# Routed attention and a SoLU MLP on one core: the first batch's fourth pair loaded in 128-byte runs and turned by VectorE

## The chip, the core and the metric

The kernel runs on one core of a Trainium2 chip: TensorE (PE, with its weight loads PEld), VectorE (DVE), ScalarE (ACT), GpSimd (POOL) and SyncE (SP), which here issues nearly all DMAs. The metric is device microseconds of one execution. The kernel before took 225.69 us, the median of three runs (225.38 to 227.81).

## What is computed

Attention over 4 batches, 8 heads, 768 tokens of 64 numbers, in which a query sees only the keys assigned to the same of 16 clusters, and then a SoLU MLP over the 3072 tokens:

```
q_assign = argmax(q_n @ c_n.T); k_assign = argmax(k_n @ c_n.T)      # 16 clusters per head
scores = where(q_assign[:, None] == k_assign[None, :], (q @ k.T) / sqrt(64), -1e9)
x = softmax(scores) @ v                                             # heads side by side: 3072 x 512
h = x @ w_in                                                        # 512 -> 1024
solu = h * softmax(h)
out = ((solu - mean) / sqrt(var + 1e-6) * g_ln) @ w_out             # 1024 -> 512
```

## The kernel before

**Work items and their written order.** The kernel records every step as a named item with an engine, a planner's cost, a due time and the items it needs (`Weave.add`, L97). The engines' queues are written out by hand as lists of kinds (`ORDER`, L28 to L73): each kind takes the next item of that kind on that engine, and `AWAY` (L74 to L91) moves single items from their default engine to another. `Weave.run` (L124) walks the queues and emits the instructions. Every engine executes its queue in order; an item whose inputs are late holds up all behind it.

**Names.** `b.p` is batch and pair of heads (4 batches, 4 pairs); a further `0` or `1` is q or k.

- `ld` loads one tensor of a pair into `raw` (eight buffers), `lv` loads v, `cv` casts it (three buffers for v, so that lv0.3 waits for cv0.0).
- A pair has to lie with the 64 numbers of a head on partitions. From batch 1 on, `load` (L396) brings 32 x 32 blocks with four DMAs, each row of a block a run of 128 bytes, and `xt` (L404) turns the blocks on DVE by one 32-wise transpose. For batch 0 (`by_token`, L351) the tokens are brought in long runs, one DMA of 1536-byte runs (`load_apart`, L372), turned on PE (`tp`, L382, three transposes of 128 x 128 each) into the PSUM region `hreg`, and copied from there by `xa` (L389) on ACT or DVE. Pair 0.0 is treated in halves (a further `.0` or `.1`).
- `ca` casts the turned tensor to bf16 into the tile `qk` (L423). `cl` multiplies it by the centroids (L438), `tb` turns the result (L456), `mx` takes the maximum over 16 (L465), `oh` compares (L474), `ot` turns the marks back (L487), `pl` copies them below q and k in `qk` (L498), and `bl` clears the rows of the other head (L521). The score matmul then contracts over the 64 numbers and the 16 or 32 marks, so that a pair of the same cluster gets a constant on top, which the exponential takes off again.
- Pairs 0.1 to 0.3 are treated "apart" (`apart`, L355): each head has its own 16 rows of marks, placed by POOL from a wide turned tile, with no `bl`.
- `S` is a bank of scores (L594, ring of three PSUM banks), `E` its exponential on ACT (L604, ring of nine `e` tiles), `V` the product with v for one head and 128 tokens (L615), `N` the division on DVE (L628). In batch 0, units 0 to 3 are pair 0 (six banks of 384 each), and then, three banks of 512 each, 4 to 7 pair 1, 8 to 11 pair 2, 12 to 15 pair 3, and 16 to 21 the last two token blocks of pairs 1, 2 and 3.
- `lo` and `li` load w_out and w_in in slabs of 512 KB; `wi` casts a slab of w_in; `su`, `sk`, `me`, `ce` sum, keep, average and centre w_out, with `lg`, `gt`, `gk`, `sg`, `gs` for g_ln.
- Per block of 128 tokens `f`: `tx` turns x (a DMA), `h` is two of its eight matmuls with w_in into `hreg`, `hm` the maximum, `ex` the exponential, `u` the product, `tu` turns u (a DMA; for the last two blocks `ptu` on PE and copies), `bn`, `ag`, `at`, `al` the statistics, `y` two of the eight matmuls with w_out, `sc` the scaling and `ou` the store. The first `h` needs tx0 and all four `wi`; tx0 needs N6.
- `wm` and `fl` are matmuls on zeros that only keep PE busy at the start; `cp` and `cq` turn the centroids, `cb` and `cf` keep them in two forms, `zo` and `z` clear or fill tiles.

**DMAs.** Each DMA on SP waits for the one eight before it (eight semaphores in turn). Nothing on SP is reordered.

Of the kernel before, what the change touches and what calls it, by code (L numbers as in the profile page):

```python
# [22 lines left out]
class Weave:  # L23
# [18 lines left out]
    """
    ORDER["PE"] = """
        wm tp2 cp tp cl tp fl5 cl fl4 S3 tp2 S2 tp S cq S tp S2 tp2 S2 V3 S cl S tp2 V3 S gt S tp S
        tp S2 cl S2 V2 S V S2 tp S2 tp S2 V2 S V S2 cl S2 V2 S V2 S3 V S2 V2 S2 V S cl S3 su S2 V3 S
        V S3 V3 S2 V S su S2 V S V3 S3 me S3 V4 S3 cl S3 V4 S2 h S h S2 h S h S2 V3 S2 V h S h V S V
        S h S V S V S h S2 V3 S2 V h S2 h V2 S y3 S2 h3 S3 y V3 h V S2 V2 S cl S3 h2 S2 V3 S y2 S V
        h2 S V y2 S h S V h S2 h S y3 S2 y V3 h S3 cl V2 S V S y S2 y2 S3 V3 S y S2 V3 S2 cl S V S2
        V2 S h S2 V2 S V S h S2 V2 cl V2 S3 y2 S V S2 V y S2 y V2 S3 h2 S V h S h S2 V h S V S V y2
        S h V y2 S2 V S h3 S cl V S2 V2 S h V cl S3 h2 V y V S3 y2 V S h V3 S y S h S2 h2 S3 V2 y h  # L50
        S V S2 y V3 y S3 h3 y S3 V3 S h S V S V cl S V S h S cl V2 S3 y V2 S y S2 y V2 S3 h y V S3 V
        h V2 S3 cl S2 V2 S y3 S2 y S V3 S V S y S2 V S V3 S2 y2 S3 y V2 S2 h V2 S3 h3 S V S2 V y S V
        h2 V2 S y S2 y V y S h2 S3 cl h V S2 V3 S h V2 S3 h2 S y S2 V h S2 V y2 V4 S3 y h S2 h V h V
# [9 lines left out]
        bn oh bn xt hm ot ag N cv u bn2 xt hm tb mx u N tb oh mx hm ot bn2 oh ag u N sc ag hm bn ot
        u bn N xt2 ag xt2 hm tb N bl mx tb bn2 oh u N xt ag xt sc hm ot tb mx oh N bn sc N u bn N ag
        xt ot bn ca N mx sc oh hm u bn ag N xt hm bn2 bl tb u ot ag N hm mx bn2 u bn N oh ot hm bl2
        u ag N cv hm sc bn u N hm ag bn N bn u bn2 hm ag2 N bn u bn2 N ag hm bn u N ag hm bn2 u bn2
        hm sc u N ag2 bn tx hm bn sc u bn ag hm bn tu ag u bn2 tu ag sc
# [101 lines left out]
def kernel(  # L169
# [11 lines left out]
    nc = tc.nc  # L181
# [241 lines left out]
    def cast(b, p, i, hh, cols, e):  # L423
        xt, h = xts[b, p, i], 2 * p + hh
        r = rows(h)
        if apart(b, p):
            src, dst = by_two(b, p, i)[r], every_other(b, p, i, hh)[:D]
        else:
            src, dst = xt[r, cols], side(b, p, i, hh, cols)[:D]
        if e == "ACT":  # L430
            nc.scalar.activation(dst, src, Act.Copy, scale=inv_C if i else 1.0)
        elif i == 0:
            VEC[e].tensor_copy(dst, src)  # L433
        else:
            VEC[e].tensor_scalar(dst, src, scalar1=inv_C, scalar2=1.0,  # L435
                                 op0=Alu.mult, op1=Alu.mult)

    def clusters(b, p, hf):  # L438
# [59 lines left out]
    def place(b, p, hf, i, part, e):  # L498
# [355 lines left out]
    add("wm", "PE", 3.55, -1000, lambda e: [idle(FF2) for _ in range(6)])  # L854
# [42 lines left out]
    for idx, (b, p) in enumerate(pairs):  # L897
        first = first_of(b, p)
        if by_token(b):
            for hf, i in ((hf, i) for hf in range(2) for i in range(2)):  # L900
# [5 lines left out]
                add(f"tp{t}.{hf}", "PE", 0.7 - 0.2 * hf if halves_of(b, p) else 0.36, first - 15 + i + hf,  # L906
# [9 lines left out]
        for i in range(2):  # L916
# [3 lines left out]
            if seq >= 8:  # L920
                pb, pp = pairs[(seq - 8) // 2]
                o = (seq - 8) % 2
                free = ([f"tp{pb}.{pp}.{o}.{x}" for x in range(2)] if by_token(pb) else
# [6 lines left out]
            elif by_token(b):  # L930
# [319 lines left out]
```

## Time and profile before

| what | value |
|---|---|
| median of three runs | 225.69 us |
| the profiled execution, its own time | 225.95 us |
| its span, from the first to the last instruction | 223.9 us |
| granted PE clock | 1.00 throughout |
| hreg<-ident_f,raw (tp, L386), 48 matmuls | 8.3 us busy |
| xt<-hreg (xa, L393), 10 on DVE and 6 on ACT | 5.1 and 2.8 us busy |
| xt<-raw (xt, L407), 24 on DVE | 22.6 us busy |
| DMA queue q1, share of 16 engines | 80.6% |
| HBM read and written | 23.11 and 6.29 MB |

Busy shares say how much of the span an engine worked; the stretches say when. A group of instructions has its line, engine, tiles and shape, then total busy time and mean ns of one, then the idle time just before them and what ended it. In the chain of waits each step was released by the one before it. First E at 10.52 us, first h at 46.16, first ex at 50.36.

### The profile page before, as it was taken

The page shows a single profiled execution, that of the slowest core. Times are in us where ns is not written, and L with a number is a line of the kernel's source. Part 1 is how long each engine was busy: PE and PEld are TensorE (multiplying, and loading weights), DVE is VectorE, ACT ScalarE, POOL GpSimd, SP SyncE. Part 2 cuts the span into 40 slices and gives each one's busy share as a digit, 9 for nine tenths or more (in the row PEclk, how much of TensorE's full clock was granted, in tenths as well). Part 3 has the DMA queues.
Part 4 walks back from the last instruction along what each step waited for, and adds up shares of the span by engine and source line. Part 5 has one row for each costly group of instructions (what it writes and reads, how often), then busy time and mean ns, then how long its engine had stood idle before and what let it go on. Part 6 is the DMA issues. An engine that isn't in the chain of part 4 may idle for free.

```text
span 223.9 us, 6574 instructions
## 1 busy us (share of the span) xinstructions
PE 215.1 (96%) x2388; PEld 148.1 (66%) x2420; DVE 197.3 (88%) x359; ACT 191.5 (86%) x371; POOL 127.1 (57%) x247
## 2 busy tenths in 40 slices
PE   7899999999999999999999999999999999999993
PEld 3576756677667678776677667777677687754442
DVE  3799899899999989999998989887998889888981
ACT  3689999999998999998889899999999998982362
POOL 3489843964794999547668634943895413031331
PEclk9999999999999999999999999999999999999999
DMA  7998989999898989999999999199931433766622
GB/s 152 353 318 147 249 199 275 290 243 158 132 199 140 232 130 165 193 189 177 183 218 168 184 195 195 65 174 232 236 64 28 79 70 120 96 146 170 176 97 94
DMA packets 125679, 38.80 MB, mean 173 GB/s; under 512 B 115016, under 2 KB 121168, under 8 KB 125648
## 3 DMA queue, kind: packets, MB, share of 16 engines
q1 hardware_dynamic: 123904, 37.87, 80.6%
q10 hardware_dynamic: 1744, 0.52, 1.0%
q8 instruction: 19, 0.31, 0.6%
q14 instruction: 12, 0.10, 0.2%
HBM read 23.11 MB, written 6.29 MB: 131 GB/s over the span
## 4 chain that ended last, share of the span: by engine, by line
PE 86%; ACT 5%; DVE 3%; issue 3%; DMA 1%; POOL 1%; ACTq 0%; DVEq 0%; POOLq 0%
PE sps L601 28%; PE hreg L710 18%; PE yps L771 16%; PE ops L624 14%; ACT e L607 5%; PE csc L450 4%; PE hreg L386 2%; PE hreg L574 1%; PE hreg L771 1%; DMA c_all<-in_centroids_dram 1%; PE csc L445 1%; DVE bs L738 1%; DVE u L727 1%; ACT xt L393 0%; PE hreg L584 0%
## 5 line engine op out<-in xcount | busy, mean ns | idle before, releaser
L607 ACT ACTIVATE e<-sps 128x512 bf16<-128x512 f32 (+1 forms) x294 | 151.0, 599 | 12.2 <-PE sps L601 10.2
L601 PE MATMUL sps<-qk 80*128 80x256 bf16 (+5 forms) x636 | 93.8, 264 | 1.8 <-POOL qk L514 0.7
L601 PEld LDWEIGHTS <-qk 80*128 80x128 bf16 (+1 forms) x636 | 60.2, 121 | 27.9 <-issue 9.0
L624 PEld LDWEIGHTS <-e 128*128 128x128 bf16 x1152 | 50.4, 97 | 12.3 <-issue 1.9
L624 PE MATMUL ops<-v,e 128*128 128x65 bf16 x1152 | 55.0, 193 | 0.1
L710 PE MATMUL hreg<-w_in_sb,xT 128*128 128x512 bf16 x173 | 49.1, 379 | 1.1
L771 PE MATMUL yps<-w_out_c,uT 128*128 128x512 bf16 x171 | 46.4, 379 | 0.6
L727 DVE TENSOR_TENSOR u<-e_sb,hreg 128x1024 bf16<-128x1024 bf16 x24 | 29.0, 1210 | 4.9 <-ACT e_sb L722 4.7
L514 POOL COPY qk<-oht 32x384 f32<-32x384 f32 (+1 forms) x50 | 24.4, 488 | 15.8 <-DVE oht L494 13.6
L738 DVE BATCH_NORM_STATS2 bs<-u 128x6 f32<-128x512 bf16 x48 | 31.5, 676 | 0.2
L716 DVE TENSOR_REDUCE nmax<-hreg 128x1 f32<-128x1024 f32 x24 | 29.0, 1209 | 2.6 <-PE hreg L710 2.2
L722 ACT ACTIVATE e_sb<-hreg,nmax 128x1024 bf16<-128x1024 f32 x24 | 26.9, 1120 | 4.5 <-DVE nmax L716 4.4
L433 POOL CAST qk<-xt 64x768 bf16<-64x768 f32 (+1 forms) x31 | 26.1, 842 | 5.5 <-DVE xt L393 3.9
L771 PEld LDWEIGHTS <-uT 128*128 128x128 bf16 x200 | 18.2, 97 | 12.3 <-DVE uT L704 0.7
L754 POOL TENSOR_SCALAR esq<-es,mv 128x1 f32<-128x1 f32 x24 | 8.5, 355 | 29.0 <-DVE mv L742 20.8
L435 POOL TENSOR_SCALAR qk<-xt 64x768 bf16<-64x768 f32 (+1 forms) x28 | 23.0, 820 | 1.7
L710 PEld LDWEIGHTS <-xT 128*128 128x128 bf16 x192 | 16.8, 97 | 9.4 <-issue 0.6
L407 DVE STREAM_TRANSPOSE xt<-raw 128x768 f32<-128x768 f32 x24 | 22.6, 953 | 0.2 <-DMA raw<-in_q_dram 0.2
L748 POOL TENSOR_SCALAR es<-esum 128x1 f32<-128x1 f32 x24 | 5.3, 221 | 27.6 <-ACT e_sb L722 27.1
L649 DVE TENSOR_TENSOR x<-ops,den 128x256 bf16<-128x256 f32 (+1 forms) x39 | 18.9, 486 | 1.3
L757 POOL TENSOR_TENSOR alpha<-esq,halves 128x1 f32<-128x1 f32 x24 | 13.5, 561 | 2.0
L786 ACT ACTIVATE y<-yps,alpha 128x512 f32<-128x512 f32 x13 | 9.0, 692 | 6.4 <-PE yps L771 6.0
(80 smaller groups left out, 170.1 us busy)
## 6 DMA issues: line engine op xcount, KB each, us to landing
vf<-in_v_dram SPq DMA_DIRECT2D x16, 384.0 KB, 4.4
out_dram<-y SPq DMA_DIRECT2D x23, 256.0 KB, 2.7
raw<-in_q_dram SPq DMA_DIRECT2D x50, 96.0 KB, 3.7
raw<-in_k_dram SPq DMA_DIRECT2D x50, 96.0 KB, 3.0
w_g<-in_moe_w_out_dram SPq DMA_DIRECT2D x4, 512.0 KB, 5.3
w_st<-in_moe_w_in_dram SPq DMA_DIRECT2D x4, 512.0 KB, 5.9
raw<-in_q_dram SPq DMA_DIRECT2D x3, 384.0 KB, 6.3
raw<-in_k_dram SPq DMA_DIRECT2D x3, 384.0 KB, 6.8
```

What stands on the lines that cost most here:

```text
L433: VEC[e].tensor_copy(dst, src)
L435: VEC[e].tensor_scalar(dst, src, scalar1=inv_C, scalar2=1.0, op0=Alu.mult, op1=Alu.mult)
L514: ins = VEC[e].tensor_copy(dst.bitcast(F32), src.bitcast(F32).unsqueeze(1) .to_broadcast([NB, 2, n // 2]))
L601: nc.tensor.matmul(sps_[n, k][:, c0:c0 + w], side(b, h // 2, 1, h % 2, keys)[r], side(b, h // 2, 0, h % 2, slice(s0 * P, s0 * P + w))[r])
L607: nc.scalar.activation(es[n, k][:, :w], sps_[n, k][:, :w], Act.Exp, scale=exp_scale, bias=-exp_scale)
L624: nc.tensor.matmul(opss[g][:, s, :VW], es[n, k][:, c0:c0 + P], v1[slot(b, h // 2)][:, h % 2, kt, :VW], start=(kt == 0), stop=(kt == n_t - 1))
L710: uses(nc.tensor.matmul(hreg[:, at(f, f2)[1], :], xTs[f][:, dc, :], w_in_sb[:, dc, f2 * FF2:(f2 + 1) * FF2], start=(dc == 0), stop=(dc == ...
L716: uses(nc.vector.tensor_reduce(ff[f, "nmax"][:], pair_of(f), axis=AXY, op=Alu.max, negate=True), *both(f))
L722: uses(nc.scalar.activation(ff[f, "e"][:], pair_of(f), Act.Exp, bias=ff[f, "nmax"][:], accum_out=ff[f, "esum"][:]), *both(f))
L727: uses(nc.vector.tensor_tensor(ff[f, "u"][:], ff[f, "e"][:], pair_of(f), op=Alu.mult), *both(f))
L738: nc.vector.bn_stats(ff[f, "bs"][:, f2, :], ff[f, "u"][:, f2, :])
L771: ins = nc.tensor.matmul(dst, ff[f, "uT"][:, at(f, f2)[0] * (n_fc // 2) + c, :], w_out_c[:, fc, cols], start=(fc == 0), stop=(fc == n_fc - 1))
```

## The change

1. Pair 0.3 is taken out of the way of batch 0 (`by_pe` is true only for pairs 0 to 2 of batch 0). It is loaded like the later batches, in eight DMAs of 32 x 32 blocks (98 KB each) instead of two of 393 KB, turned on DVE by two `xt` instead of twelve PE transposes and four copies, and treated with 32 rows of marks and a `bl` instead of apart. Its tokens keep the order of batch 0: its `ca` and its `cl` read every sixth column of the turned tile. (The old helper `by_pe` is renamed `by_product`.)
2. `pl` of pair 0.0 may also run on ACT; three of them do (pl0.0.0.1.1, pl0.0.1.0.0, pl0.0.1.0.1).
3. All five written orders and the list `AWAY` are new. One `fl` less stands on PE (8 for 9). `sk` goes to ACT, `wi3` to DVE, three more `sc` to ACT, four more `pl` of batches 2 and 3 to SP.

The beginnings of the orders, with the kinds resolved to items:

```
SP   before: ld0.0 (4) lv0.0 si ld0.1.0 ld0.1.1 ld0.2.0 ld0.2.1 lv0.1 lg ld0.3.0 ld0.3.1 ld1.0.0.0 ld1.0.0.1
             lv0.2 lv0.3 ld1.0.0.2 ld1.0.0 ld1.0.1.0 ld1.0.1.1 lo0 lo1 ... lo2 ... lo3 ... ld1.1.1 li0-3 tx0
SP   after:  ld0.0 (4) lv0.0 si lv0.1 ld0.1.0 lg ld0.1.1 ld0.2.0 lv0.2 ld0.2.1 ld0.3.0.0-2 lo0 ld0.3.0
             ld0.3.1.0-2 ld0.3.1 ld1.0.0.0-1 lo1 ... lo2 ... lo3 ld1.1.0.2 ld1.1.0 lv0.3 ... ld1.1.1 li0-3 tx0
DVE  before: cn cb xa0.0.0.1 ca0.0.1.0.0 tb0.0.0 mx oh ot pl0.0.0.1.1 pl0.0.0.0.0 tb0.0.1 mx oh ot xa0.1.0.0 ...
DVE  after:  cn cb tb0.0.0 mx oh ot pl0.0.0.1.0 pl0.0.0.0.0 tb0.0.1 mx oh ot pl0.0.1.1.0 xa0.1.0.0 xa0.1.0.1
             xa0.1.1.0 xa0.1.1.1 cf tb0.1 mx oh ot gk N0 xa0.2.0.1 xa0.2.1.0 pl0.1.0.0 xt0.3.0 xt0.3.1 tb0.2
             mx oh ot N1 tb0.3 cv0.2.1 pl0.2.1.1 N2 xt1.0.0 xt1.0.1 mx0.3 N3 oh0.3 ot0.3 tb1.0 ...
ACT  before: wa xa0.0.0.0 xa0.0.1.0 ca0.0.0.0.0 ca0.0.0.1.1 xa0.0.1.1 ca0.0.1.0.1 ca0.0.1.1.0 E0.0 (9 E)
             E1.3 E1.4 E1.5 xa0.2.1.0 xa0.2.1.1 (6 E) xa0.3.0.0 E3.0 ...
ACT  after:  wa xa0.0.0.0 xa0.0.1.0 xa0.0.0.1 xa0.0.1.1 ca0.0.0.0.1 pl0.0.0.1.1 ca0.0.1.1.0 E0.0 (9 E)
             pl0.0.1.0.0 pl0.0.1.0.1 E1.3 E1.4 E1.5 xa0.2.0.0 (8 E) xa0.2.1.1 E3.2 ... E13.0 sk E13.1 ...
POOL before: po z1 ca0.0.0.0.1 ca0.0.0.1.0 pl0.0.0.1.0 pl0.0.0.0.1 cv0.0.1 z2 bl0.0.0 ...
POOL after:  po ca0.0.0.0.0 ca0.0.0.1.0 ca0.0.0.1.1 ca0.0.1.0.0 zo pl0.0.0.0.1 bl0.0.0 ca0.0.1.0.1 cv0.0.0 ...
PE   before: ... S0.0 S0.1 S0.2 tp0.1.0.0 tp0.1.0.1 S1.0 S1.1 tp0.1.1.0 S1.2 cq ... S13.1 su1 ... S15.1 me
             ... S19.0 h0.0.0 ... y22.0 y22.1 ptu23.0 ptu23.1 y22.2 y22.3 y23
PE   after:  ... S0.0 S0.1 S0.2 cq S1.0 tp0.1.0.0 S1.1 S1.2 tp0.1.0.1 ... S13.0 su1 S13.1 S13.2 S14.0 me
             ... S19.1 h0.0.0 ... y22.0 y22.1 y22.2 ptu23.0 ptu23.1 y22.3 y23
```

At the end ACT copies both halves of u23 (before, DVE copied the second, behind bn23), and DVE both of u22.

The diff without the orders, cut to its core:

```diff
+    def by_pe(b, p):
+
+        return by_token(b) and p < 3
+
     def apart(b, p):
-        return by_token(b) and not halves_of(b, p)
+        return by_pe(b, p) and not halves_of(b, p)
...
         if apart(b, p):
             src, dst = by_two(b, p, i)[r], every_other(b, p, i, hh)[:D]
+        elif by_token(b) and not by_pe(b, p):
+            src = xt[r].rearrange("p (n t) -> p t n", t=n_t)
+            dst = side(b, p, i, hh, cols)[:D].rearrange("p (t n) -> p t n", t=n_t)
...
-            nc.tensor.matmul(csc[c * NB:(c + 1) * NB, :n], c_bd[:, p, :],
-                             xts[b, p, i][:, lo + part * n:lo + (part + 1) * n],
+            x = xts[b, p, i][:, lo + part * n:lo + (part + 1) * n]
+            if by_token(b) and not by_pe(b, p):
+                x = xts[b, p, i][:].rearrange("p (n t) -> p t n", t=n_t)[
+                    :, part * (n_t // 2):(part + 1) * (n_t // 2)]
+            nc.tensor.matmul(csc[c * NB:(c + 1) * NB, :n], c_bd[:, p, :], x,
                              tile_position=(0, c * NB))
...
+        elif e == "ACT":
+            ins = nc.scalar.copy(dst, src.unsqueeze(1).to_broadcast([NB, 2, n]))
...
-        if by_token(b):
+        if by_pe(b, p):
             for hf, i in ((hf, i) for hf in range(2) for i in range(2)):
...
-            elif by_token(b):
+            elif by_pe(b, p):
                 add(f"ld{t}", "SP", 0.55, first - 40 + i,
                     (lambda e, b=b, p=p, i=i: load_apart(b, p, i)),
...
-            if by_token(b):
+            if by_pe(b, p):
                 kept = [[f"xa{t}.{hf}"] for hf in range(2)]
```

Three of the planner's costs change with it (`wm`, `tp` of pair 0.0, `pl` on ACT); the queues are written out, so these move no instruction.

More of the change, by code (lines that the diff above doesn't have):

```diff
@@ L63 @@
[L63 to L67, printed above, removed]
+        cn cb tb mx oh ot pl2 tb mx oh ot pl xa4 cf tb mx oh ot gk N xa2 pl xt2 tb mx oh ot N tb cv
@@ L999 @@
                 e = ("DVE", "POOL")[j % 2] if half else "POOL" if apart(b, p) else "SP"
-                costs = ({"DVE": 0.3, "POOL": 0.41} if half else
+                costs = ({"DVE": 0.3, "POOL": 0.41, "ACT": 0.42} if half else
                          {"POOL": 0.76, "DVE": 0.46} if apart(b, p) else
```

98 lines of the change are left out of this document (51 added, 47 removed).

## The prediction

> **What bounds the kernel now.** I read the page's busy times first, then the busy times by stretch, the waits of the first 50 us, the chain of waits around the first scores, the groups by form and last the timelines around the first `h`.
>
> ```profile
> PE 215.1 (96%) x2388; PEld 148.1 (66%) x2420; DVE 197.3 (88%) x359; ACT 191.5 (86%) x371; POOL 127.1 (57%) x247
> ```
>
> PE is the bound over the whole span. But the shares are an average. By stretch (columns: the stretch, its length, PE, weight loads, DVE, ACT and POOL busy with their instructions, clock, DMA share, GB/s):
>
> ```profile
> 10.00:15.00 5.00, 4.84 (x53) 3.98 (x57) 4.74 (x13) 3.76 (x10) 4.03 (x12) 1.00 1.11 356
> 20.00:25.00 5.00, 4.71 (x66) 3.40 (x66) 4.67 (x11) 4.89 (x12) 4.62 (x10) 1.00 0.74 214
> 45.00:50.00 5.00, 4.94 (x69) 3.82 (x68) 4.82 (x9) 5.00 (x11) 3.31 (x6) 1.00 1.24 261
> 80.00:85.00 5.00, 4.95 (x68) 4.07 (x66) 4.80 (x8) 4.75 (x11) 4.52 (x9) 1.00 0.79 125
> ```
>
> From 15 to 60 us ACT runs exponentials at 92 to 100% of the time, and a busy PE there is partly one that waits inside overlapping matmuls: from 20 to 30 us it issued 39 score matmuls, 84 of V, 6 transposes and one `cl`; at the chain's paces (0.11 a score of 256 columns and 0.17 of 384, 0.032, 0.11, 0.78) that is 4.5 + 2.7 + 0.7 + 0.8 = 8.7 of 10 us. So up to about 50 us, while no MLP work is there, ACT sets the pace; after that PE does (4.95 of 5, ACT with gaps). What ACT waited for between 10 and 50 us:
>
> ```profile
> POOL w_in_sb L552 <- DMA w_st<-in_moe_w_in_dram: 4.1, 1, 4.1
> ...
> ACT e L607 <- PE sps L601: 2.2, 6, 1.1
> ...
> ACT e L607 <- PE ops L624: 0.7, 1, 0.7
> ...
> ACT xt L393 <- PE hreg L386: 0.4, 1, 0.4
> ```
>
> Of the 2.2 us, 1.1 lie before the first E (10.52). The rest, 1.1 + 0.7 + 0.4 = 2.2 us, is ACT's whole idle time from E0.0 to ex0 (50.36). The chain into the first scores (start, us, what):
>
> ```profile
> 6.85 0.56 DVE xt L393
> 7.40 0.26 DVE qk L435
> 7.66 0.30 DVE cst L459
> ...
> 9.35 0.37 POOL qk L514
> 9.72 0.05 issue
> 9.77 0.35 POOL qk L514
> 10.12 0.04 issue
> 10.16 0.65 PE sps L601 x3
> 10.81 0.66 PE hreg L386 x6
> ```
>
> DVE's copy and cast stand ahead of the first tb, and two placings run one behind the other on POOL. Forms used below (busy us, mean ns):
>
> ```profile
> L607 ACT ACTIVATE e<-sps 128x512 bf16<-128x512 f32 x270 | 141.2, 607 | 10.3 <-PE sps L601 9.1
> L407 DVE STREAM_TRANSPOSE xt<-raw 128x768 f32<-128x768 f32 x24 | 22.6, 953 | 0.2 <-DMA raw<-in_q_dram 0.2
> L514 POOL COPY qk<-oht 32x384 f32<-32x384 f32 x44 | 22.3, 507 | 14.4 <-DVE oht L494 12.4
> L393 ACT COPY xt<-hreg 128x384 f32<-128x384 f32 x6 | 2.8, 477 | 1.3 <-PE hreg L386 1.3
> ```
>
> **The change, part by part.** The profiled execution took 225.95 us (span 223.9, 2.05 around it, taken as unchanged), 0.26 above the median of 225.69; the sum is made against 225.95.
>
> *Head.* The first cl ends at 6.74 + 0.53 = 7.27; tb, which starts at 7.59 behind the copy and cast, can start at 7.30 now that ACT copies and POOL casts: -0.3. The four first placings go to DVE (two at 0.29), ACT and POOL (one each). In the old order POOL's pair ends 0.9 us after ot; now DVE's pair ends last at 0.6: -0.3. ot would end at 8.9 and S0.0 start at 9.55. ACT then casts ca0.0.1.1.0 (0.52) before E0.0, which starts near 10.0 instead of 10.52. POOL must be through four casts (0.53 each, the third behind ACT's copy at 7.33) and `zo` (0.41 by POOL's memset of the same width, L523), at about 9.0, just in time. I take -0.5; bounds 0 (POOL late) and -0.6.
>
> *Pair 1 behind lv0.1.* ld0.1.0 is issued behind lv0.1, its transfer of 393 KB (1.05 us at the 375 GB/s of 8 to 14 us) first. Old issue 4.01 and 5.1 to landing give 9.1, now 10.2; PE gets to it after S0.0 to S0.2, cq and S1.0, near 10.3. 0, bounds 0 and +0.5; what would stall behind it is S1.1, whose E is due at 11.2.
>
> *ACT from E0.0 to ex0.* The same 76 exponentials. One copy less (-0.47). Two placings, pl0.0.1.0.0 and .1: no ACT row has this shape; nearest are ACT's copy (0.48) and its cast of 64x384 (0.52), and POOL's placing of half the width (0.35), so 0.45 each, +0.9. They stand where E1.3 waits for V0 (a ring of nine e tiles): the 0.72 us of the second wait above hide all but 0.2. `sk` moves from DVE (0.69) to ACT, between 0.52 (an E of as many columns) and 0.69: +0.6, with the PE-made `me` right behind it. Of the remaining 1.4 us of ACT waits, tb0.1 at 14.4 to 15.2 instead of 15.9 and fewer transposes ahead of scores should save about 0.3. Sum -0.47 + 0.2 + 0.6 - 0.3 = 0; bounds -1.4 (all idle gone) and +1.2 (none saved, placings not hidden).
>
> *PE.* Twelve transposes go, three in 0.33 us on the chain: 1.3 us, and one dummy matmul (0.1). They lie where ACT sets the pace, so I count 0 beyond the 0.3 above; bounds 0 and -1.4. The cl of pair 3 now reads every sixth f32. Strided weight loads of L601 take 127 ns against 97 in batch 0: with the same ratio 0.78 becomes 1.02, 0 to +0.25, under ACT's pace 0.
>
> *DVE and POOL for pair 3.* DVE gets two xt (0.95 each) for three copies (0.54), an ot of 0.56 instead of 0.97, three placings fewer, one `bl` more: nearly even. POOL gets four placings at 0.51 where it had one. In the new order xt0.3.1 stands ahead of tb0.2 and waits for eight small loads. From the landing of ld0.2.1 (14.4 as the old ld0.3.0) I get 8 x 0.62 (below) + 1.4 for lo0 = 20.8; tb0.2 then runs at 21.8, ot0.2 ends at 24.0, pl0.2 by 26; S8.0 is due at 27. The placings of pair 3 end at 34.4 (ot0.3 at 32.2, four of 0.51 in a row), S12.0 is due at 33.5 to 34.5; in the old order it ran at 34.5. So 0, bounds 0 and +1.0.
>
> *DMA and SP.* Two loads of 393 KB (2.1 us together) become eight of 98 KB in 128-byte runs. Between 80 and 85 us, with little else than such loads in flight, the queue moved 125 GB/s at a share of 0.79, 158 GB/s at full share: 0.62 us each, 5.0 together, so +2.9 us of DMA time, and six more issues of 0.5 on SP, all ahead of lo and li. Against it lv0.3 moves behind ld1.1.0; where it stood SP waited 2.3 us for cv0.0. li thus comes 0.6 to 2.9 us later; I take 0.6, as the DMA share of 0.74 in 20 to 25 us shows the gap that SP's wait left. The cover:
>
> ```profile
> 39.59 1.04 POOL L552 CAST w_in_sb<-w_st 128x1024 bf16<-128x1024 f32 x1 [4.13 <-DMA w_st<-in_moe_w_in_dram]
> ...
> 42.57 3.00 POOL L552 CAST w_in_sb<-w_st 128x1024 bf16<-128x1024 f32 x3
> ```
>
> wi3 ends at 45.57 and the first h starts at 46.16: 0.6 us. So 0 here, upper bound +2.3 (rival B).
>
> *After 50 us.* All counts on PE are equal. PE has 1% of gaps there, so a new order can win little and lose by new waits (the old ACT waits for scores after 50 us: 8.1 us in 21, 0.8 at most). Three y scalings move from DVE (0.73) to ACT (0.69): 2.1 us, and ACT has some 0.25 us free in each 5. At the end PE waited 0.34 us for u23 with y22.2 and y22.3 still to do; y22.2 now fills it, and both copies of u23 stand on ACT, so that y23 need not wait behind bn23: -0.3 to -0.5. I take -0.3; bounds -0.5 and +1.5.
>
> Sum: -0.5 + 0 + 0 + 0 + 0 + 0 - 0.3 = -0.8, so 225.95 - 0.8 = 225.15, say 225.2.
>
> **The rivals.** A: *the transposes count in full.* For it: PE stands without a gap in the chain from 10.16 to 16.4. Against it: ACT's 4.89 of 5 from 20 on. 225.2 - 1.4 - 0.3 (the rest of ACT's gaps) = 223.5.
>
> B, the other side: *the w_in slabs come late.* At +2.9 us of DMA, wi3 ends near 48.5; h0.0.0, due at 46.2, stops PE's queue 2.3 us, with V and S behind it, ACT runs dry after three banks (1.5 us), and PE has no slack later: 227.5; with small loads at 0.8 us (four issued in 3.18 at 80.08) it is 1.4 more, 228.9. It decides once the last slab is cast after 46.2. For it: the 4.1 us wait above. Against it: the wait at lv0.3 that goes.
>
> C: *POOL's strided casts of pair 3 delay its first scores.* The four casts read every sixth f32; the row is 0.83 with packed reads. With the 31% of the weight loads they cost 1.0 more, hidden by POOL's wait for ot0.3 (2.3 us); at double their cost, 3.3, S12.0 is 1.0 late: 226.2. [...]
>
> D: *the new order brings two or three waits of 0.8 after 50 us:* 226.8 to 227.6.
>
> [...]
>
> **How the numbers follow.** Forecast 0.47 (own range 224.2 to 226.2), A 0.16, B 0.17, C 0.07, D 0.13. 1% of 225.69, about what a measurement can tell from no change, is 2.26: faster below 223.43 is half of A and a little of the forecast's tail, 0.11; slower above 227.95 is two thirds of B and some of D, 0.16; within 0.73. Half of A's lower part (0.08) and half of B with D's tail (0.11) are left out by 223.1 to 228.3.
>
> **What would show it.** Right: S0.0 near 9.55, E0.0 near 10.0, no ACT gap before E1.3, ex0 within 0.5 of 50.36, y23 0.3 us closer to u23. Wrong: PE waiting at the first h with wi behind a DMA (B), ex0 a microsecond or more earlier (A), S12.0 waiting for POOL (C), new ACT waits after 60 us (D), or S0.0 waiting for POOL's casts.

## The result, and the profile after

The changed kernel took 229.47 us (median of six, 229.04 to 230.71) beside 225.74 for the kernel before: ratio 1.0162, 95% interval 1.0131 to 1.0193, slower by 3.7 us. The prediction was 225.2, with 223.1 to 228.3 as its range. The profiled execution of the changed kernel took 229.53 us, its span 227.5. Executions more than 1.5% above the fastest of their kernel (two of e1, two of e8) are left out of all ratios below, while medians and ranges are of all.

The page's busy times of the changed kernel:

```profile
PE 218.7 (96%) x2407; PEld 146.7 (64%) x2407; DVE 197.7 (87%) x350; ACT 194.2 (85%) x375; POOL 130.1 (57%) x247
```

PE is busy 3.6 us longer with twelve transposes fewer, which by itself shows nothing: the trace before has records of 173 and 171 matmuls of `h` and `y`, this one of 192 and 184. A matmul of V takes 193 ns in both, one of scores of 256 columns 274. The same stretches as before, and one more, 34 to 38 us (columns as in the prediction):

```profile
10.00:15.00 5.00, 4.86 (x51) 3.51 (x44) 4.20 (x11) 4.66 (x12) 3.73 (x12) 1.00 1.11 314
20.00:25.00 5.00, 4.80 (x64) 2.83 (x67) 4.87 (x9) 4.84 (x12) 4.63 (x7) 1.00 1.06 208
...
34.00:38.00 4.00, 2.85 (x35) 1.31 (x33) 3.73 (x9) 2.30 (x6) 3.71 (x5) 1.00 1.15 217
45.00:50.00 5.00, 4.63 (x70) 3.39 (x69) 4.93 (x10) 4.99 (x11) 2.08 (x2) 1.00 1.03 210
80.00:85.00 5.00, 5.00 (x66) 3.35 (x64) 4.55 (x10) 4.82 (x10) 2.16 (x5) 1.00 0.99 154
```

In the first and the last of them little has changed, and from 45 to 50 us PE has lost 0.3. But from 34 to 38 us ACT, which sets the pace there, works 2.30 of 4 us (3.96 in the kernel before), and PE 2.85 (3.87). The same stretch in the kernel before:

```profile
34.00:38.00 4.00, 3.87 (x54) 2.27 (x52) 3.54 (x8) 3.96 (x8) 1.46 (x2) 1.00 0.94 228
```

ScalarE's timeline in the changed kernel (start, us, group, and in brackets the idle time before it and what ended that; lines between left out):

```profile
11.05 3.56 ACT L619 ACTIVATE e<-sps 128x384 bf16<-128x384 f32 x9 [0.30 <-PE sps L613]
14.63 1.03 ACT L524 COPY qk<-oht 32x384 bf16<-32x384 bf16 x2
15.68 1.26 ACT L619 ACTIVATE e<-sps 128x384 bf16<-128x384 f32 x3
...
26.92 8.72 ACT L619 ACTIVATE e<-sps 128x512 bf16<-128x512 f32 x17 [1.18 <-PE sps L613]
...
37.94 2.06 ACT L619 ACTIVATE e<-sps 128x512 bf16<-128x512 f32 x4 [1.32 <-PE sps L613]
40.12 0.59 ACT L592 COPY w_sum<-hreg 128x512 f32<-128x512 f32 x1
...
53.43 1.11 ACT L734 ACTIVATE e_sb<-hreg,nmax 128x1024 bf16<-128x1024 f32 x1
```

ex0 starts at 53.43 instead of 50.36. The last `u` starts 3.48 us later than before, so 3.1 of 3.5 us are lost by ex0. Between the first E and ex0, added up from this view and the same of the kernel before, whose two longest gaps there are these:

```profile
14.80 1.25 ACT L607 ACTIVATE e<-sps 128x384 bf16<-128x384 f32 x3 [0.72 <-PE ops L624]
16.44 0.86 ACT L393 COPY xt<-hreg 128x384 f32<-128x384 f32 x2 [0.39 <-PE hreg L386]
```


| us | before | after |
|---|---|---|
| E0.0 starts | 10.52 | 11.05 |
| ScalarE idle (gaps of 0.15 and more) | 2.15 | 3.22 |
| its copies, placings, `sk` | 1.20 | 2.27 |
| its 76 exponentials, with pauses under 0.15 | 36.49 | 36.89 |
| ex0 starts | 50.36 | 53.43 |

The waits of 9 to 54 us (total, times, longest):

```profile
ACT e L619 <- PE sps L613: 3.5, 6, 1.3
POOL w_in_sb L564 <- DMA w_st<-in_moe_w_in_dram: 2.4, 3, 1.0
PEld L636 <- DVE x L661: 2.1, 3, 1.4
...
PE ops L636 <- DVE x L661: 1.8, 3, 1.1
```

The last two are V waiting for N on VectorE; in the kernel before, one such wait of 0.3 us is listed. What stood ahead of N on VectorE and PE in those places, and on POOL beside it, is in these lines of the timelines of PE, VectorE and POOL:

```profile
24.63 1.54 PE L461 MATMUL csc<-xt,c_bd 128*32 128x384 f32 x8
...
31.31 0.87 PE L461 MATMUL csc<-xt,c_bd 128*32 128x384 f32 x8
...
37.07 0.55 PE L636 MATMUL ops<-v,e 128*128 128x65 bf16 x12 [1.15 <-DVE x L661]
```
```profile
32.18 1.86 DVE L494 TENSOR_TENSOR oh<-cst,mx 128x384 bf16<-128x384 f32 x1
...
35.74 0.72 DVE L494 TENSOR_TENSOR oh<-cst,mx 128x384 bf16<-128x384 f32 x1
```
```profile
22.98 0.82 POOL L440 CAST qk<-xt 64x768 bf16<-64x768 f32 x1
...
28.78 3.20 POOL L440 CAST qk<-xt 64x768 bf16<-64x768 f32 x2
32.05 3.44 POOL L442 TENSOR_SCALAR qk<-xt 64x768 bf16<-64x768 f32 x2
```

The `cl` of pair 0.3, with its strided operand, takes 1.54 us where that of pair 1.0 takes 0.87. POOL's strided casts take 1.58 and 1.69 each (means) where the packed one takes 0.82. And oh0.3 on VectorE, which begins 0.13 us behind the third of them, takes 1.86 where oh1.0 takes 0.72; N4, which V10.0 waits for at 37.07, stands behind it.

The chain of waits into the first scores (those at 11.59 are S1.0's; the matmuls of S0.0 to S0.2 begin at 10.68):

```profile
7.97 0.39 DVE cst L469
...
9.70 0.19 POOL qk L526
...
10.60 0.51 POOL qk L442
11.11 0.46 POOL v L544
...
11.59 0.32 PE sps L613
```

VectorE's copy and cast are gone from it, as forecast, and POOL's queue takes their place. In this execution PE also waited 0.68 us for the first load of k; in nine of the ten experiments with this head E0.0 starts between 9.72 and 10.25, in e15 at 10.59.

Last, SyncE's queue: start and length of its issues in the kernel before and in the changed one.

```profile
7.48 0.39 SPq L374 DMA_DIRECT2D raw<-in_q_dram  x1
7.92 0.58 SPq L374 DMA_DIRECT2D raw<-in_k_dram  x1
...
21.46 1.04 SPq L399 DMA_DIRECT2D raw<-in_k_dram  x2
...
33.72 3.89 SPq L549 DMA_DIRECT2D w_st<-in_moe_w_in_dram  x4
```
```profile
8.19 4.38 SPq L403 DMA_DIRECT2D raw<-in_q_dram  x3
...
15.26 4.06 SPq L403 DMA_DIRECT2D raw<-in_k_dram  x4
...
22.20 5.20 SPq L403 DMA_DIRECT2D raw<-in_k_dram  x4
...
38.33 3.15 SPq L561 DMA_DIRECT2D w_st<-in_moe_w_in_dram  x4
```

The two long loads of pair 0.3 were issued in 1 us; the eight short ones hold SyncE for 11 us, with one lo between. The last load of pair 1.0 is issued at 27.4 instead of 22.5, the last slab of w_in at 41.5 instead of 37.6.

### The profile page after: what moved, and what is told of

It is laid out like the page before. It is cut to its first block, busy times and chain, and to the rows that moved or that the text cites. A ratio compares the mean times of both kernels' runs of the same rounds, so it can differ in the third digit from the quotient of the medians.

```text
span 227.5 us, 6596 instructions
## 1 busy us (share of the span) xinstructions
PE 218.7 (96%) x2407; PEld 146.7 (64%) x2407; DVE 197.7 (87%) x350; ACT 194.2 (85%) x375; POOL 130.1 (57%) x247
## 4 chain that ended last, share of the span: by engine, by line
PE 83%; DVE 6%; ACT 3%; DMA 3%; SPq 2%; issue 1%; POOL 1%; DVEq 0%; ACTq 0%; POOLq 0%
PE sps L613 26%; PE hreg L722 18%; PE yps L783 16%; PE ops L636 14%; PE csc L461 4%; DMA raw<-in_k_dram 3%; PE hreg L390 2%; SPq L403 2%; ACT e L619 1%; DVE oh L494 1%; DVE u L739 1%; ACT e_sb L734 1%; PE hreg L783 1%; DVE xt L411 1%; PE csc L452 1%
## 5 line engine op out<-in xcount | busy, mean ns | idle before, releaser
L613 PEld LDWEIGHTS <-qk 80*128 80x128 bf16 (+1 forms) x636 | 61.0, 121 | 29.2 <-issue 11.8
L722 PE MATMUL hreg<-w_in_sb,xT 128*128 128x512 bf16 x192 | 52.9, 379 | 0.1
L783 PE MATMUL yps<-w_out_c,uT 128*128 128x512 bf16 x184 | 49.5, 379 | 0.0
L526 POOL COPY qk<-oht 32x384 f32<-32x384 f32 (+1 forms) x46 | 23.1, 503 | 16.6 <-DVE oht L504 12.7
L442 POOL TENSOR_SCALAR qk<-xt 64x768 bf16<-64x768 f32 (+1 forms) x32 | 28.4, 887 | 4.0 <-DVE xt L411 2.0
L411 DVE STREAM_TRANSPOSE xt<-raw 128x768 f32<-128x768 f32 x26 | 24.4, 956 | 0.4 <-DMA raw<-in_k_dram 0.2
L722 PEld LDWEIGHTS <-xT 128*128 128x128 bf16 x192 | 16.1, 97 | 9.5 <-DVE u L739 1.6
L544 POOL CAST v<-vf 128x384 bf16<-128x384 f32 x26 | 12.7, 505 | 7.3 <-DMA vf<-in_v_dram 6.8
L798 ACT ACTIVATE y<-yps,alpha 128x512 f32<-128x512 f32 x16 | 11.1, 691 | 5.4 <-PE yps L783 3.6
```

What stands on the lines that cost most here:

```text
L411: nc.vector.transpose(xt[:], raws[b, p, i][:].rearrange("p j c -> p (j c)"))
L442: VEC[e].tensor_scalar(dst, src, scalar1=inv_C, scalar2=1.0, op0=Alu.mult, op1=Alu.mult)
L613: nc.tensor.matmul(sps_[n, k][:, c0:c0 + w], side(b, h // 2, 1, h % 2, keys)[r], side(b, h // 2, 0, h % 2, slice(s0 * P, s0 * P + w))[r])
L722: uses(nc.tensor.matmul(hreg[:, at(f, f2)[1], :], xTs[f][:, dc, :], w_in_sb[:, dc, f2 * FF2:(f2 + 1) * FF2], start=(dc == 0), stop=(dc == ...
L783: ins = nc.tensor.matmul(dst, ff[f, "uT"][:, at(f, f2)[0] * (n_fc // 2) + c, :], w_out_c[:, fc, cols], start=(fc == 0), stop=(fc == n_fc - 1))
```

## The experiments

Three theories, named in the expectations by number where they have one: the strided reads of pair 0.3 on POOL and PE (T1), the short loads through DMA (T2, rival B), and VectorE's written order, in which N1 and N4 stand behind work that is late (T4). All ratios are to the kernel before, in the same set of runs.

| kernel | median (range) | ratio (95%) |
|---|---|---|
| e1_packed | 230.24 (227.57 to 231.6) | 1.0162 (1.0118 to 1.0207) |
| e2_long_runs | 229.61 (229.5 to 230.68) | 1.0181 (1.0153 to 1.0208) |
| e3_packed_long | 228.24 (227.57 to 228.61) | 1.0108 (1.0083 to 1.0132) |
| e4_before_strided | 227.03 (226.87 to 227.93) | 1.0067 (1.0042 to 1.0092) |
| e5_n1_early | 229.89 (229.32 to 230.32) | 1.0182 (1.0162 to 1.0202) |
| e6_packed_n1_early | 229.3 (229.23 to 229.61) | 1.016 (1.0147 to 1.0174) |
| e7_before_head | 226.84 (226.46 to 227.34) | 1.0051 (1.0034 to 1.0068) |
| e8_before_small | 229.63 (226.75 to 232.1) | 1.0122 (1.0076 to 1.0168) |
| e9_before_dve_turn | 226.13 (225.7 to 227.24) | 1.0004 (0.9975 to 1.0032) |
| e10_packed_long_light_act | 231.91 (231.21 to 232.15) | 1.0246 (1.0206 to 1.0285) |
| e11_before_tail | 225.77 (225.32 to 228.63) | 0.9999 (0.9967 to 1.003) |
| e12_before_dve_turn_small | 231.75 (230.67 to 233.08) | 1.025 (1.0202 to 1.0298) |
| e13_small_unblocked | 229.55 (228.32 to 231.42) | 1.0143 (1.0074 to 1.0213) |
| e14_new_unblocked | 234.64 (232.54 to 235.51) | 1.0344 (1.0284 to 1.0404) |
| e15_new_unblocked_sk | 232.99 (232.57 to 235.52) | 1.0309 (1.0246 to 1.0372) |
| e16_small_dummies | 230.97 (229.16 to 232.27) | 1.0191 (1.013 to 1.0252) |
| e17_small_later | 229.87 (229.61 to 232.98) | 1.0204 (1.015 to 1.0258) |
| e18_packed_long_sk | 228.34 (228.0 to 228.59) | 1.0097 (1.0065 to 1.0128) |

**The strided reads and the short loads, each undone.** e1 loads rows six tokens apart, so that the turned tile is read packed; e2 brings each tensor of pair 0.3 in one long-run load; e3 does both. e4 puts only the strided reads into the kernel before.

```diff
 # e1 and e3: cast and cl lose their strided branch; e1's load, for pair 0.3:
+                in_=SRC[i][b, 2 * p + c // 2, :, (c % 2) * NB:(c % 2 + 1) * NB]
+                .rearrange("(n i t) c -> i t n c", i=NB, t=n_t))
 # e2 and e3: one load for four
+            if c == 0:
+                eng.dma_start(out=..., in_=SRC[i][b, 2 * p:2 * p + 2]
+                              .rearrange("h (p t) d -> p h (t d)", p=P))
 # e4, in the kernel before
+            if p == 3:
+                src = xt[r].rearrange("p (n h t) -> p h t n", h=2, t=n_t // 2)
```

> The changed kernel, with the eight loads of pair 0.3 fetching each block's 32 rows six tokens apart (still 128-byte runs, as many of them), so that the turned tile lies in the order in which cast and cluster product read it, and both read packed. Nothing else differs. Theory T1 (the strided reads: POOL's four casts at 1.57 to 1.80 us instead of 0.83, cl0.3 at 1.47 instead of 0.78, DVE's oh0.3 held up to 1.86 beside a strided cast): casts back to 0.83, oh0.3 to 0.57, ACT's gaps before units 6 and 12 (1.18 and 1.70) down to about 0.3 each, ex0 2.3 us earlier, 227.2 us (226.6 to 227.8). Rival T2 (late transfers: xt1.0.1 waiting for ld1.0.1, w_in late): 229.5, N4 still late. Rival T3 (the written order itself): 229.5 with the gaps in place.

> The changed kernel, with pair 0.3 loaded by one DMA of 1536-byte runs per tensor in place of four of 128-byte runs, as the kernel before loads it; the strided reads stay. The tokens and columns of pair 0.3 then stand in the wrong places, so the output of that pair is another. T1: no change, 229.5 (229.0 to 230.0), casts still 1.6 us. T2: DMA time of 2.9 us saved, xt1.0.1 and w_in earlier, 227.0 to 227.5. T3: 229.5.

> Both at once: long runs for pair 0.3, and cast and cluster product reading packed (contents of pair 0.3 in the wrong places). T1: as with packed reads alone, 227.2, less at most 0.5. T2: as with long runs alone, 227.0 to 227.5, casts of no account. If both count, 225.5 or less. T3: still over 228.5.

> The kernel before, with the casts and the cluster product of pair 0.3 reading every sixth column of their tile, and nothing else changed (the tokens of that pair end up in another order). T1: the four casts take 1.6 us instead of 0.83; POOL waited 2.65 us for ot0.3 there, which hides most, cl0.3 0.7 longer on PE: 0.5 to 1.5 us slower than before, 226.2 to 227.2. T2 and T3: 225.7, no change.

e4 came as expected: 1.5 us from strided reads alone. Its timeline of ScalarE has the two gaps of the changed kernel, smaller:

```profile
26.92 5.50 ACT L612 ACTIVATE e<-sps 128x512 bf16<-128x512 f32 x11 [0.84 <-PE sps L606]
...
38.23 1.57 ACT L612 ACTIVATE e<-sps 128x512 bf16<-128x512 f32 x3 [0.81 <-PE sps L606]
```

But by its median neither e1 nor e2 is faster than the changed kernel; only e3 is, by 1.2 us. With packed reads (e3) the casts take 0.84 and 0.86, `cl` 0.85 and oh0.3 0.76, and no gap before ex0 exceeds 0.48. In the profile of e1 (an execution of 231.53 us) other waits open, and PE's granted clock falls (to 0.50 from 28 to 36 us). Of e1's six executions the one with a mean granted clock of 1.00 took 227.57 us, which is what T1 had said; the other five, with 0.975 to 0.985, took 229.54 to 231.6. So packed reads alone may be worth 1.9 us where the clock holds, but that rests on one execution. T1 and T2 are each true in part, and one hides the other.

**VectorE's order.** N1 directly behind tb0.2, in the changed kernel (e5) and in e1 (e6).

```diff
-        ... pl xt2 tb mx oh ot N tb cv
+        ... pl xt2 tb N mx oh ot tb cv
```

> The changed kernel, with N1 directly behind tb0.2 on DVE instead of behind mx0.2, oh0.2 and ot0.2; nothing else differs. Theory T4 (the new written order puts the divisions N1 and N4 behind longer runs of DVE work than DVE gets done, V4.0 and V10.0 wait for them at the head of PE's queue, ACT runs dry, and in some runs PE's clock falls to half for some 11 us after the idle time): the gap before unit 6 falls from 1.2 to under 0.4, 228.3 to 228.8 us. T1 (strided reads) alone: the gap stays at 0.7 or more, because cl0.3 is as long as before, 229.2 to 229.6. T2 (late transfers): 229.5.

> Packed reads for pair 0.3 (loads six tokens apart) and N1 directly behind tb0.2. T1 and T4 together: both gaps of ACT under 0.4, no fall of the clock, 226.5 to 227.3, and runs within 0.5 of each other. T2: still 229 or more. If the order costs beyond N1 and N4 it stays above 227.5.

Both missed: the waits moved. In e5 the gap before unit 6 stays (1.20), so N1 is not what makes it (the strided cl0.3, 1.55 us on PE, stands ahead of those scores), and the later one grows to 1.86; in e6 the wait moves to cl0.3, which waits 1.4 us for tb0.2 (one bank for both), behind an xt0.3.1 that waits 1.3 us (as I read it, for its last short load).

**Head, tail and turn, each alone in the kernel before.** e7 has the head of the change; e11 its last blocks; e9 turns pair 0.3 by two xt, with long loads and packed reads, and loses the twelve transposes and four copies.

```diff
 # e7, ACT
-        wa xa2 ca2 xa ca2 E12 xa2
+        wa xa4 ca pl ca E9 pl2 E3 xa2
 # e11, PE (and both copies of u23 on ACT)
-        ptu2 y6 ptu2 y6
+        ptu2 y7 ptu2 y5
 # e9, DVE and ACT (tp of pair 0.3 leave PE, bl0.3 goes to DVE)
-        pl mx xa2 oh xa cv N
+        pl mx xt oh xt cv N
-        ca2 E12 xa2 E6 xa E58
+        ca2 E12 xa2 E64
```

> The kernel before, with the head of the change alone: pair 0.0's copies on ACT, its casts on POOL, its marks placed by DVE, ACT and POOL, pl0.0.1.0.0 and .1 on ACT before E1.3; loads and all else as before. My head term: E0.0 0.5 us earlier; the two placings fill ACT's wait before E1.3 and cost 0.3; 225.0 to 225.4 against 225.5. If head placement is no gain (PE's first transposes and clock set it): 225.5 to 226.0.

> The kernel before with the change's last blocks alone: y22.2 ahead of the turning of u23, both copies of u23 on ScalarE, both of u22 on VectorE. Forecast's term of the tail, -0.3: 225.2 to 225.5, with y23 starting 0.3 us closer behind u23 than before's 1.71 us after its end. Rival, no gain: 225.5 to 225.9.

> The kernel before with part 1 of the change alone and without its two prices: pair 0.3 comes in one load of 1536-byte runs per tensor at the old place, is turned by two xt on VectorE where its copies stood, read packed, marked with 32 rows, a bl and the old three engines of its pl; its tokens lie in wrong places. Forecast's terms PE 0 and DVE 0 (twelve transposes off PE, four copies for two xt, the wide ot for a narrow one): 225.2 to 226.2, ex0 within 0.4 of 50.36. Rival A (the transposes count): 223.8 to 224.8, ex0 near 49. Rival: two xt in VectorE's queue delay N1 or tb0.3 by themselves: 226.5 to 227.5, a ScalarE gap of 0.6 or more before unit 6 or 12.

e7 missed: E0.0 starts at 9.72, 0.8 earlier, but the units from 26 us on run 0.2 behind before, and the time is 1.1 us longer. Its timeline of ScalarE:

```profile
13.70 1.03 ACT L514 COPY qk<-oht 32x384 bf16<-32x384 bf16 x2
15.26 1.26 ACT L609 ACTIVATE e<-sps 128x384 bf16<-128x384 f32 x3 [0.53 <-PE ops L626]
```

The two placings were to stand in the 0.72 us wait for V0. 0.53 of that wait is still there behind them. e11 gives nothing: both copies of u23 one behind the other on ACT take 1.07 us and end at 218.60, where the two engines' ended at 218.70. e9 came as expected: ratio 1.0004. ex0 is 0.5 earlier, but so is E0.0 in that execution (9.98): from E0.0 to ex0 it takes 39.87 us, and the kernel before 39.84. The transposes were worth next to nothing, and rival A is out.

**The short loads in the old order.** e8 is the kernel before with the loads of pair 0.3 split into 128-byte runs, turned on PE as before; e12 is e9 with e1's short loads.

```diff
 # e8
+                    in_=SRC[i][b, 2 * p + hh].rearrange("(p t) d -> p t d", p=P)[
+                        :, :, x * NB:(x + 1) * NB])
```

> The kernel before, with the two loads of pair 0.3 split into four each of 128-byte runs, in the same place on SP; PE still turns them and nothing else differs. T2 (and rival B of the prediction): 2.9 us more DMA time ahead of lo and li, wi3 ends 1 to 3 us later, the first h waits 0.5 to 2.3, 226.0 to 228.0. T1 and T4: no change, 225.3 to 225.8.

> As the kernel before with pair 0.3 turned by VectorE and read packed, but with each tensor of pair 0.3 in four loads of 128-byte runs (rows six tokens apart, all tokens in their right places). Theory that the small loads cost through VectorE's queue (xt0.3.1 and xt1.0.1 wait for them, tb and N stand behind): 227 to 230, with VectorE's xt waiting over 1 us for raw and a ScalarE gap of 1 us or more. Rival, the loss of the kernel before with small loads lay in PE's transposes standing ahead of scores and waiting for the last load: within 0.5 of the long-run version.

Both cost more than their theories had said: e12 is 5.6 us above e9, and e8, forecast at 226.0 to 228.0, scatters from 226.75 to 232.1. In both, SyncE's queue ends later (last slab of w_in at 40.2 in each, 36.5 in e9, 37.6 in the kernel before), and the waits of e12 show where it bites:

```profile
DVE xt L417 <- DMA raw<-in_k_dram: 3.2, 1, 3.2
...
PE csc L461 <- DVE xt L417: 2.4, 1, 2.4
```

xt1.0.1 waits 3.2 us for the last load of pair 1.0, and cl1.0, whose result nobody needs before S22, stands on PE ahead of S9.2 and waits with it. Then PE's granted clock falls, to 0.50 from 34 to 38 us (stretches of e12, clock in the third column from the right):

```profile
30.00:32.00 2.00, 0.54 (x4) 0.00 (x0) 0.09 (x1) 0.81 (x2) 0.00 (x0) 1.00 0.35 54
32.00:34.00 2.00, 1.06 (x4) 0.19 (x4) 1.93 (x5) 0.00 (x0) 0.00 (x0) 0.56 0.86 255
34.00:36.00 2.00, 2.00 (x12) 0.94 (x14) 1.94 (x4) 0.92 (x2) 1.29 (x2) 0.50 1.35 183
36.00:38.00 2.00, 2.00 (x10) 0.28 (x3) 1.10 (x2) 0.65 (x2) 1.75 (x3) 0.50 0.97 291
38.00:40.00 2.00, 2.00 (x33) 1.79 (x31) 0.10 (x1) 1.40 (x3) 0.00 (x0) 0.74 0.93 176
```

**Taking the block away, and keeping PE busy.** e13 is e12 with xt1.0.x and cl1.0 behind nearer work; e17 moves xt1.0.1 and cl1.0 further still; e16 is e12 with 40 dummy matmuls ahead of cl1.0.

```diff
 # e13 against e12: DVE, PE
-        N xt mx xt N oh ot tb pl2 ca N pl bl xt mx N sk
+        N mx N oh ot pl2 xt N pl bl xt tb ca xt mx N sk
-        S9.1 cl1.0 S9.2 ... S12.1 V10.0
+        S9.1 S9.2 ... S12.1 cl1.0 V10.0
 # e17: DVE ... N5 sk xt1.0.1 tb1.0 ...; PE ... S13.2 cl1.0 S14.0
 # e16
+        for _ in range(40) if (b, p) == (1, 0) else ():
+            nc.tensor.matmul(csc[:, :P], ident_b[:], ident_b[:])
```

> The kernel before with pair 0.3 turned by VectorE from 128-byte loads and read packed (231.75 us in the run above), and now xt1.0.0 and xt1.0.1 behind oh0.3, ot0.3 and N4 on VectorE and cl1.0 three units later on PE (behind S12.1); the DMAs and their order are the same. Theory that the late small loads cost only by what stands behind the waiting xt: 225.6 to 227.2, no ScalarE gap above 0.8 between E0.0 and ex0, clock 0.99 or more. Rival, the DMA time itself (w_in's slabs late for the first h, or other loads late): 228 or more.

> As the unblocked kernel (229.55 us), with xt1.0.1 behind N5 and sk on VectorE and cl1.0 behind S13.2 on PE, so that neither stands where ld1.0.1 is still on its way. Theory of the block: the gap of 2.4 us before unit 12 or 13 goes, ex0 as far behind E0.0 as in the kernel before (39.8 to 40.5 us), 226.0 to 227.5. Rival, the w_in slabs (last cast near 49 us) are late for the first h and PE waits there instead: 228.3 or more, with a PE wait of 1 us or more at L724 or a ScalarE gap near 48 to 51 us.

> The kernel before with pair 0.3 turned by VectorE from 128-byte loads (231.75 us in the run above), with 40 dummy matmuls of 128 columns (some 2.2 us) ahead of cl1.0 on PE, which fill its wait for xt1.0.1. Theory that the granted clock falls because PE stood idle: clock 1.00 throughout, ScalarE's second gap (1.69 before 38.34) gone, 229.0 to 230.3. Rival, the clock falls for another reason: 0.5 again around 33 to 38 us, 231.3 to 232.5.

e13 wins 2.2 us of the 5.6 by the medians (the intervals just touch) and misses its forecast: cl1.0 still waits 0.8 for an xt1.0.1 that now stands behind N4, and the stretch of 36 to 38 us has PE busy 1.19 of 2. e17 is no better: SyncE's lateness also reaches su1, whose eight matmuls take 1.80 us instead of 1.07 while w_out's last slab lands, and sk and xt1.0.1 stand behind it. So the theory holds for part of the loss, and the rest, as I read the traces, is more work in written places that the loads, now some 3.6 us later, no longer meet. e16: the clock stays at 1.00 behind the wait:

```profile
34.00:36.00 2.00, 1.98 (x14) 0.81 (x18) 1.93 (x5) 0.72 (x2) 0.30 (x1) 1.00 1.08 272
36.00:38.00 2.00, 2.00 (x39) 1.38 (x32) 1.91 (x4) 1.82 (x4) 1.85 (x4) 1.00 1.15 181
```

From E0.0 to ex0 it takes 43.4 us and e12 45.6; E0.0 starts 1.2 later in its profile, and the medians differ by 0.8 only, with intervals that overlap, and e16's is above what was expected. The mean granted clock is 0.985 to 0.993 in the six executions of e12 and 0.991 to 1.00 in those of e16. In the profile of e12 the clock fell to 0.50 behind PE's 2.41 us of idle time, and in that of e16, with dummies in its place, it stayed at 1.00: that the idle time lowered it, at a price of about 2 us, rests on these two profiles.

**The new order without the block, and ScalarE's added work.** e14 is e6 with xt0.3.1, xt1.0.x, cl0.3 and cl1.0 further back; e15 is e14 with sk on VectorE. e10 and e18 are e3 with less on ScalarE: e10 gives sk and the two placings of pair 0.0 back, e18 only sk, to an earlier place.

```diff
 # e14 against e6, DVE (cl0.3 behind V5.1, cl1.0 behind S12.1 on PE)
-        pl xt2 tb N mx oh ot tb cv pl N xt2 mx N oh ot tb mx oh N
+        pl xt tb N mx oh ot xt cv pl tb N mx oh ot N xt bl N xt tb cv2 N mx oh
 # e10, e18: ACT; DVE
-        E9 pl2 E3 xa E8 xa E32 sk E24
+        E12 xa E8 xa E56                  # e10;  e18: E9 pl2 E3 xa E8 xa E56
-        bl xt bl ca cv2 N ca xt ce2
+        bl xt bl ca cv2 N ca sk xt ce2    # e10;  e18: bl xt cv N sk cv bl ca2 xt ce2
```

> The change with packed reads of pair 0.3 (rows six tokens apart, 128-byte loads as in the change), N1 directly behind tb0.2, xt0.3.1 behind ot0.2, xt1.0.0 and xt1.0.1 behind N3 and N4 on VectorE, cl0.3 behind V5.1 and cl1.0 behind S12.1 on PE, the w_in casts earlier on GpSimd. Theory of the block: 226.3 to 227.5, ex0 51.0 to 51.9, no ScalarE gap of 1 us. Rival, the new order loses elsewhere: 228.5 or more.

> As the unblocked new order, with sk on VectorE directly behind N5 instead of on ScalarE. Theory that ScalarE's work before ex0 counts in full: 0.4 to 0.7 less than without it (ex0 earlier by as much). Rival, sk on VectorE makes me and PE wait as it did behind ca1.0.1.0: 0.5 more or worse.

> The packed-and-long kernel (the change with pair 0.3 in one long-run load per tensor and packed reads, its tokens in wrong places), and besides sk back on VectorE behind N5 and pl0.0.1.0.0 and .1 back on GpSimd. Theory that ScalarE's extra work (placings 1.03, sk 0.48 us) is what the packed-and-long kernel still loses: ex0 0.8 to 1.4 earlier than its 51.32, time 227.0 to 227.5. Rival, the new written order's own waits: 228.0 to 228.6, with ex0 within 0.4 of 51.32.

> The packed-and-long kernel (228.24 us), with sk on VectorE directly behind N5, which stands earlier (behind xt1.1.0 and cv0.3.0). Theory that sk on ScalarE counts in full: ex0 near 50.7 against 51.32, 227.4 to 227.9. Rival, me and V wait for VectorE instead: 228.2 or more.

e14 missed by far, and e15 with it (1.6 us less, intervals overlapping): now VectorE reaches xt1.1.1 late, cl1.1 keeps PE waiting 2.5 us for it, and ScalarE has a gap of 3.94 us at 47 us (2.50 in e15). e10 tells nothing of sk, since it stood behind a cast and me kept PE waiting 2.6 us for it; but up to 37.9 us it shows that the two placings back on POOL win nothing (the 52nd E ends at 37.88, in e3 at 37.70, with the waits for V0 and the transposes back). e18 missed: sk off ScalarE, 0.48 us, and the time is that of e3; new gaps of 0.47, 0.26 and 0.27 stand in its place.

The trace of e3 shows a likely reason. From E0.0 to ex0 it takes 41.38 us (39.84 before): its gaps are fewer (1.66 against 2.15 us), ScalarE's other items take 1.06 more, and the exponentials with their short pauses 0.97 more. Over 20 to 50 us the fullest of the three engines is no longer PE or ScalarE but VectorE, the third of the busy times (first line the kernel before, second e3):

```profile
20.00:50.00 30.00, 29.25 (x389) 19.73 (x389) 27.36 (x53) 28.66 (x59) 20.12 (x32) 1.00 1.00 241
20.00:50.00 30.00, 27.83 (x355) 17.53 (x353) 28.98 (x55) 27.74 (x55) 20.07 (x30) 1.00 0.84 211
```

In e3's chain of waits every step from 35.63 us to the end of hm0 is VectorE's, one item directly behind the other, wi3 among them, which the change took from POOL; hm0 is what ex0 (51.32) needs. Three of these steps:

```profile
39.63 0.84 DVE qk L445
...
46.79 0.60 DVE w_in_sb L564
...
50.01 1.22 DVE nmax L728
```

PE's last matmul of h0 ends at the same time as VectorE's item ahead of hm0 (49.9), but the first h starts only as wi3 ends (47.35 and 47.39), so PE, too, appears to wait for VectorE there. e18 puts `sk` on this queue, and ex0 starts 0.37 later. That VectorE's queue holds ex0 in e3 is read from the chain; no run takes wi3 or other work off it. A full VectorE alone is no proof: in e9, which loses nothing, it is busy 28.43 of these 30 us.

## Why the prediction was wrong, step by step

The term that failed is *ACT from E0.0 to ex0*: put at 0, with +1.2 as its upper bound, it measured +2.5 of the 3.7 us. Its -0.3 for ScalarE's other idle time came to +1.8, because before unit 6 the scores stood behind the long strided cl0.3 on PE, and before unit 12 behind V10.0, which waited for N4. Behind that stand two terms that were put at 0: the strided reads, and the order on VectorE, which was called nearly even.

- *DMA and SP: 0, upper +2.3.* Wrong in size and place. Its sum had +2.9 us of DMA time and six issues of 0.5, and I took 0.6 because a wait at lv0.3 would go. Measured, li is issued 3.9 us later than before and the last load of pair 1.0 4.9 later; the short loads alone make 3.7 of the one (e12 against e9). The place was wrong too: rival B looked at w_in's slabs before the first h, where wi3 had 0.6 us of cover. But what comes first on the late queue is ld1.0.1, and xt1.0.1 and cl1.0 stand in front of urgent work in strictly ordered queues. In the old order that costs 5.6 us. The new order is written for the later loads (its xt1.0.1 waits 0.2 us), so the changed kernel does not pay it there. Rival B's time (227.5 to 228.9) comes near the 229.47 measured, but not by its path: the last slab, issued at 41.1, lands by 48.2, wi3 starts at 48.78 behind other work of VectorE, and PE shows no gap at the first h (49.45). In e2, with long loads, the last slab is issued 2.0 us earlier than in the kernel before, and nothing is won.
- *DVE and POOL for pair 3, and the cl of pair 3: 0, bounds 0 to +1.0.* Failed in its sizes. I took the strided read of `cl` for +0.25 from the ratio of strided weight loads; it was +0.67, and not hidden. Rival C had the casts at double cost, 1.0 us late at S12.0, with a chance of 0.07. They did double (0.82 to 1.58 and 1.69), but S12.0 was not the place: beside the cast on POOL oh0.3 took 1.1 us longer on VectorE, and N4 and V10.0 came later with it. The sum took VectorE as nearly even and had no term for wi3 (0.69) there; from 20 to 50 us it is busy 28.85 us instead of 27.36. In the old order the reads cost 1.5 us (e4).
- *ACT from E0.0 to ex0: 0, bounds -1.4 and +1.2.* Measured +2.5: the idle time was to fall by 0.3 beside the wait that the placings fill, 0.72. Without that wait it rose by 1.8 (3.22 against 1.43). ScalarE's own work rose by 1.07, as its parts had it (0.9 + 0.6 - 0.47). The hiding of the placings came nearly right in the changed kernel: E1.3 starts 4.63 us behind E0.0 instead of 4.28, 0.35 more where the sum had 0.2. In e7, with the rest of the old order, it does not (5.54).
- *Head: -0.5.* Right for E0.0 by the middle of the profiles (9.94 in eleven with the new head, 10.52 in nine with the old one; each group scatters over 1.3 us), wrong as a gain: by 26 us nothing of it is left (e7).
- *PE: 0.* Right: e9.
- *After 50 us: -0.3.* Small miss: 0 (e11). The rest after ex0 is +0.4. In the kernels that keep the old order the delay at the first `u` is still there at the last, within 0.25 us (2.85 and 2.86 in e13; -0.51 and -0.27 in e9), so there nothing lost before 50 us is made good.
- *Sum.* The parts, measured alone in the old order, add up to 8.2 us (5.6 + 1.5 + 1.1) and the change costs 3.7. The parts overlap, and the new order avoids one of them. With short loads and strided reads both undone it still costs 2.4 us (e3), in which sk on ScalarE (e18) and, up to 38 us, the placings (e10) do not show as single causes. In e3's profile 1.0 us of it is there at ex0, behind a chain of VectorE's work, and the rest comes after. Which items of the new order make up those 2.4 us stays open; wi3 on VectorE is untested. No variant beat the kernel before.

## What to carry to other kernels

Where queues run in a written order, cost a load by what its place in the issuing queue does to all loads behind it, and then look on every engine for the first item that waits for one of those, and for what stands behind that item. Bound an access pattern that the trace does not show by its worst row, and list the instructions that run beside it on other engines. Moving one item off a full queue won nothing here while a neighbouring queue was as full (e18): take the moved item's price as moved, not as gone, and follow the chain of waits to see which queue is the full one.

## What the runs showed of the hardware

- PE's granted clock fell to 0.50 behind these waits of PE: 2.41 us in e12 (0.50 from 34 to 38 us; the four matmuls of cl1.0 behind the wait took 1.50 us, the four ahead of it 0.84), 1.63 us in e1 (0.50 from 28 to 36) and 2.47 us in e14 (0.50 from 46 to 48). Behind one of 1.15 us in the changed kernel it stayed at 1.00. From what length on a wait lowers it, these runs do not show.
- A compare on VectorE with two inputs, oh0.3, took 1.86 us beside a strided cast on POOL; oh1.0, beside none, took 0.72, and oh0.3 of e3, beside a packed cast, 0.76. In e2 and e5 it is the next compare, oh1.0, that takes 1.77 and 1.79; oh0.3 of e2, begun 0.11 ahead of such a cast, takes 0.55, and the cast 1.88 instead of 1.58. In the changed kernel the cast that began at 32.05 took 1.58 and ended near 33.6, oh0.3, begun at 32.18, ended at 34.04, and the next cast took 1.80. As I read these times the two hold each other up; how they do it is not shown.
- An f32 operand read every 24 bytes: means of 1.58 and 1.69 us against 0.82 on POOL (64x768), 1.54 against 0.87 for eight matmuls.
